# Attention-bias kernel on one core: zero fills, parameter transfer, distance sign and coefficient columns at the start rearranged

## Chip, cores and metric

The kernel runs on 1 core of one Trainium2 chip. The metric is the device time of one launch in microseconds (us), and the time of a kernel is the median of its runs. Times inside the program are counted from the start of the profiled span.

## What is computed

Attention with a learned relative-position bias, followed by two feed-forward stages. Sizes: batch 2, 8 heads, 576 positions, head size 64, hidden width 32 of the bias network, then 1152 tokens by 512 features and 2048 inner features.

```python
scores = scale * np.matmul(q, k.transpose(0, 1, 3, 2))
psi_rel = np.log1p(np.abs(pos[:, None] - pos[None, :]))
psi_i = np.log1p(np.maximum(pos[:, None], 1.0))
x = (psi_rel / psi_i)[..., None]
h = np.maximum(x @ w1 + b1, 0.0)
scores = scores + (h @ w2).transpose(2, 0, 1)[None]
attn = softmax(scores)
x = attn @ v                        # then to (tokens, features)
h = x @ w_in;  x = (P(h) / Q(h)) @ w_out        # first feed-forward stage
h = x @ w_in2; out = np.maximum(0.01 * h, h) @ w_out2
```

## The kernel before

**Stages.** The program first makes the bias for all heads and positions ("bias stage", up to about 85 us), then runs attention unit by unit over (head pair, batch), then the two feed-forward stages on TensorE. The order of every engine's work is written out by hand in lists (`BIAS_PLAN`, `EXTRA`, `PLAN`, `TAIL`, `START`) or computed before the launch by a planner (`plan_first`); no list depends on measured time. The change touches what comes ahead of the first mask, and the two calls that make the bias columns.

**How the bias is made.** For a hidden unit the ReLU is linear on either side of one distance, so the kernel turns it into a comparison of a signed distance with a threshold. A table `z` (128 x 1152, f16) holds distances for 32 hidden units in each of 4 partition groups; it is loaded by ACT's queue (L613) and multiplied by the sign `sg` of the hidden weight on ScalarE (L628). The thresholds `thr` and `nthr` (128 x 144) come from a short chain on VectorE: `sg` (L626, L627), `aw`, `rate` (L629 to L633), `thr` (L652, L653), an Exp on ScalarE (L654), then `thr` and `nthr` (L655, L656).

For each of the 36 row groups n, `b_mask` makes 4 masks (one for each c) from `z`: on VectorE with `thr` (L689), or on ScalarE with `nthr` (L687), as the letters of `MASKS[n % 4]` say ('A' for ScalarE). `b_mm` multiplies masks by the coefficients `coef` on TensorE into two PSUM tiles (L697). `b_t0` on ScalarE (L709) scales the first by `rows_e` and adds a column of `ca_i`; `b_t1` on GpSimd (L715) multiplies by `te`; `b_out` on VectorE (L720) adds the second and a column of `cab`, and SyncE's queue writes the tile to its place (L723). `BIAS_PLAN` orders these for each n; masks run 3 to 4 groups ahead.

**The parameters.** One transfer on SP's queue (L611) brings `par`, 128 rows of 348 f32 (174 KB): `wc` (2 columns), `wflat` (32), `w2rep` (128), the feed-forward scalars (6), `rows_z` (144) and `rows_e` (36). Behind it on that queue are the two halves of `te` (L614, L615) and `sm` (L616). From `wc` GpSimd makes `nwc` and `hwc` (L635, L637). ScalarE makes four pieces of `c32` (L647) and their f16 part `coef` (L648); GpSimd makes the rest (L649). One small matmul fills `psc` (L641).

**`cab` and `ca_i`.** `cab` (128 x 4 x 2) is zeroed on GpSimd (L639). `cab_constants()` runs on VectorE between the first VectorE masks and the rest: for each of the 4 mask patterns it copies the ScalarE quarters out of `psc` (6 copies in all, L670) and multiplies `rows_e` by a column (4 times, L671).

**The zero fills.** Two tiles `qz` of 128 x 2 x 1152 hold the queries of a unit, with zeros where a head's rows meet the other head's columns. GpSimd writes these zeros with four fills of 64 x 1152 (L660, L661), issued in program order behind the coefficient work, and then `ones`, `tiny` and `ln15` (L662 to L664). The queries are put in by `prep_q`, later in the bias stage.

Of the kernel before, what the change touches and what calls it, by code (L numbers as in the profile page):

```python
# [9 lines left out]
F32 = mybir.dt.float32  # L10
# [16 lines left out]
MASKS = ('AVVA', 'VVVA', 'VVAA', 'VVVA')  # L27
# [88 lines left out]
HI_MERGED = ()  # L116
LO_MERGED = ()
REM_MERGED = (0, 1)
PAR = 168 + S // 4 + NG
GROUPS = [[(0, 0), (0, 1)], [(1, 0), (1, 1)], [(3, 0), (3, 1)], [(2, 0), (2, 1)], [(8, 2)]]  # L120
GROUPS_END = [[(0, 0), (0, 1)], [(1, 0), (1, 1)], [(3, 0), (3, 1)], [(2, 0), (2, 1)], [(8, 2)]]
GROUPS_0 = [[(2, 0), (2, 1)], [(0, 0), (0, 1)], [(1, 0), (1, 1)], [(3, 0), (3, 1)], [(8, 2)]]
# [145 lines left out]
def host_constants():  # L268
    psi = np.log1p(np.arange(S, dtype=np.float32))
    psi_i = np.log1p(np.maximum(np.arange(S, dtype=np.float32), np.float32(1.0)))  # L270
    p = np.arange(128)
    c = np.arange(2 * S)
    g = p // HID
    e = p // H

    def away(off):
        return np.abs(c[None, :] - S - off[:, None])

    dist = away(4 * g).astype(np.float16)
    tabs = psi[np.minimum(away(4 * e), S - 1)].astype(np.float32)  # L280
    first = np.array([first_row(n) for n in range(NG)])
    first_z = (first[:, None] + 16 * np.arange(4)[None, :]).reshape(-1)
    rows_z = psi_i[4 * g[:, None] + first_z[None, :]]
    rows_e = np.float32(1.0) / psi_i[4 * e[:, None] + first[None, :]]
    eye = np.eye(128)
    m = np.concatenate([np.arange(8), [-1, 8, -1]]).repeat(64)
    k = np.arange(128)[:, None]
    rows = np.concatenate([rows_z, rows_e], 1).astype(np.float32)
    small = np.concatenate([eye, k == m[None, :]], 1).astype(np.float32)
    return rows, {  # L290
        "dist": np.ascontiguousarray(dist),
        "tabs": np.ascontiguousarray(tabs),
        "small": np.ascontiguousarray(small),
    }
# [3 lines left out]
def attn_bias_moe_kernel(  # L298
# [16 lines left out]
    V, A, G, PE, SP = nc.vector, nc.scalar, nc.gpsimd, nc.tensor, nc.sync  # L315
# [285 lines left out]
    with ExitStack() as st:  # L601
# [3 lines left out]
        psa = st_s.enter_context(tc.tile_pool(name="psa", bufs=2, space=PSUM, side="right"))  # L605
        psb = st.enter_context(tc.tile_pool(name="psb", bufs=2, space=PSUM))

        pr = b1p.tile([128, PAR], F32, name="par")
        z = b1p.tile([128, 2 * S], F16, name="z")
        te = b1p.tile([128, 2 * S], F32, name="te")  # L610
        SP.dma_start(out=pr, in_=par)  # L611
        halves = (slice(512, 2 * S), slice(0, 512))
        A.dma_start(out=z, in_=dist)  # L613
        SP.dma_start(out=te[:, halves[0]], in_=tabs[:, halves[0]])  # L614
        SP.dma_start(out=te[:, halves[1]], in_=tabs[:, halves[1]])  # L615
        SP.dma_start(out=sm, in_=small)  # L616
        wc, wflat, w2rep = pr[:, 0:2], pr[:, 2:34], pr[0:HID, 34:162]
        rows_z, rows_e = pr[:, 168:168 + S // 4], pr[:, 168 + S // 4:PAR]

        def col1(nm):
            return b1p.tile([128, 1], F32, name=nm)

        sg, aw, rate = col1("sg"), col1("aw"), col1("rate")
        V.tensor_scalar(sg, wc[:, 0:1], 0.0, 2.0, ALU.is_ge, ALU.mult)  # L626
        V.tensor_scalar(sg, sg, -1.0, None, ALU.add)  # L627
        A.activation(z, z, AF.Copy, scale=sg)  # L628
        V.tensor_scalar(aw, wc[:, 0:1], sg, 1e-30, ALU.mult, ALU.max)  # L629
        V.reciprocal(aw, aw)  # L630
        V.tensor_tensor(rate, sg, wc[:, 1:2], ALU.mult)
# [3 lines left out]
        G.tensor_scalar(nwc, wc, -1.0, None, ALU.mult)  # L635
        hwc = b1p.tile([128, 2], F32, name="hwc")
        G.tensor_scalar(hwc, wc, -0.5, None, ALU.mult)  # L637
        cab = b1p.tile([128, len(MASKS), 2], F32, name="cab")
        G.memset(cab, 0.0)  # L639
        psc = psa.tile([128, 1024], F32, tag="A", name="psc")  # L640
        PE.matmul(psc[:, 0:2], w2rep, hwc[0:HID, :], start=True, stop=True)  # L641

        coef = b1p.tile([128, 2, 2, 2, 4 * H], F16, name="coef")
        c32 = b1p.tile([128, 2, 2, 4 * H], F32, name="c32")
        for m, src in enumerate((nwc, hwc)):
            for j in range(2):
                A.activation(c32[:, m, j], wflat, AF.Copy, scale=src[:, j:j + 1])  # L647
        A.activation(coef[:, :, :, 0], c32, AF.Copy)  # L648
        G.tensor_tensor(coef[:, :, :, 1], c32, coef[:, :, :, 0], ALU.subtract)  # L649
        thr = b1p.tile([128, S // 4], F32, name="thr")  # L650
        nthr = b1p.tile([128, S // 4], F32, name="nthr")
        V.tensor_scalar(thr, rows_z, rate, 7.3, ALU.mult, ALU.min)  # L652
        V.tensor_scalar(thr, thr, -13.2, None, ALU.max)  # L653
        A.activation(thr, thr, AF.Exp)  # L654
        V.tensor_scalar(thr, thr, -1.0, sg, ALU.add, ALU.mult)  # L655
        V.tensor_scalar(nthr, thr, -1.0, None, ALU.mult)  # L656
        ca_i = b1p.tile([128, len(MASKS), NG], F32, name="ca_i")

        for u in range(2):
            G.memset(qz[u][0:64, :, S:2 * S].bitcast(F32), 0.0)  # L660
            G.memset(qz[u][64:128, :, 0:S].bitcast(F32), 0.0)  # L661
        G.memset(ones, 1.0)  # L662
        G.memset(tiny, 1e-30)
        G.memset(ln15, float(15 * np.log(2)))  # L664

        def cab_constants():
            for x in range(len(MASKS)):
                for y in range(4):
                    if MASKS[x][y] == "A":
                        V.tensor_copy(cab[32 * y:32 * y + 32, x], psc[32 * y:32 * y + 32, 0:2])  # L670
                V.tensor_scalar(ca_i[:, x], rows_e, cab[:, x, 0:1], None, ALU.mult)  # L671

        def late_constants():
            V.memset(onep, 1.0 + 1e-6)
            A.activation(ab, pr[:, 162:168], AF.Copy)
            A.activation(babs, ab[:, 4:6], AF.Abs)
            V.tensor_scalar(nab, ab[:, 0:4], -1.0, None, ALU.mult)

# [599 lines left out]
```

## Time and profile before

| | before |
|---|---|
| median of 3 runs | 681.64 us (679.17 to 682.61) |
| profiled execution, its own time | 683.32 us |
| its span | 681.5 us |
| mean granted TensorE clock | 0.96 |
| busy share of the span: PE, DVE, ACT, POOL | 88%, 77%, 59%, 55% |

PE is TensorE, DVE is VectorE, ACT is ScalarE, POOL is GpSimd, SP is SyncE. A busy share is a mean over stages that have different limits. A row of the timeline gives the start, the length, engine, line and operation, what it writes and reads, how many instructions are merged in it, and in brackets the idle time in front of it with what ended that. The granted clock is 1.00 for the upper of TensorE's two levels (2.4 GHz) and 0.50 for the lower (1.2 GHz).

### The profile page before, as it was taken

Reading aid. Unit: us, or ns where it says so; the run is one execution under the profiler, and the core shown is the slowest. Engines: PE = TensorE matmul, PEld = TensorE weight load, DVE = VectorE, ACT = ScalarE, POOL = GpSimd, SP = SyncE. Lnnn points to the kernel's source line nnn. Section 1 sums busy time; section 2 is a strip of 40 time slices with the busy share of each in tenths; the row PEclk is TensorE's granted clock in tenths of the full one; section 3 lists DMA queues with packets and bytes.
Section 4 is the critical chain, followed back from the end, with each engine's and each line's share of the span. In section 5 each row is a group of like instructions: output and inputs, shape, how many; then the busy total and the mean of one; then the engine's idle time right before and its main releaser. Section 6 shows DMA issues by size and latency. Waiting matters only on the chain.

```text
span 681.5 us, 11805 instructions
## 1 busy us (share of the span) xinstructions
PE 599.9 (88%) x4595; PEld 530.3 (78%) x4595; DVE 527.4 (77%) x815; ACT 402.4 (59%) x614; POOL 376.8 (55%) x276
## 2 busy tenths in 40 slices
PE   2777678998888877579999999999999999999998
PEld 1343467777677876579999898999999999998876
DVE  6999788888789857988999999899355465645463
ACT  5999677786687556688576776854244323232210
POOL 4678667787688711456556575853055534453340
PEclk9999889898999887779999999999999999999999
DMA  2666769999999931213211311011033312230113
GB/s 87 176 178 153 202 127 199 201 207 172 188 200 201 199 105 65 92 63 114 72 63 63 123 63 63 31 60 66 15 118 115 124 63 91 94 125 31 55 54 124
DMA packets 104359, 77.35 MB, mean 113 GB/s; under 512 B 86512, under 2 KB 86896, under 8 KB 104304
## 3 DMA queue, kind: packets, MB, share of 16 engines
q1 hardware_dynamic: 100704, 68.97, 40.1%
q10 hardware_dynamic: 3600, 7.64, 3.8%
q8 instruction: 36, 0.59, 0.4%
q14 instruction: 19, 0.16, 0.1%
HBM read 42.38 MB, written 2.36 MB: 66 GB/s over the span
## 4 chain that ended last, share of the span: by engine, by line
PE 43%; DVE 26%; ACT 11%; DMA 8%; issue 7%; POOL 3%; ACTq 1%; SPq 0%; DVEq 0%; POOLq 0%
PE ph L426 19%; PE pz L1049 13%; DMA et<-hl 6%; PE py L1008 6%; ACT mk L687 2%; DVE raw L387 2%; DVE raw L385 2%; DVE raw L383 2%; POOL hl L854 2%; DVE ph L479 2%; DVE bias L1020 2%; ACT t L709 2%; DVE s L500 2%; DVE qq L470 2%; DVE pt L801 2%
## 5 line engine op out<-in xcount | busy, mean ns | idle before, releaser
L426 PE MATMUL ph<-bias,bias 128*128 128x384 f32 x1152 | 217.8, 344 | 15.8 <-DVE s L500 13.2
L426 PEld LDWEIGHTS ph<-bias,bias 128*128 128x128 f32 x1152 | 208.8, 194 | 21.3 <-issue 13.2
L854 POOL TENSOR_TENSOR hl<-ex,hl 128x512 f16<-128x512 f32 (+2 forms) x105 | 105.1, 1018 | 34.0 <-DVE hl L841 17.7
L521 POOL TENSOR_TENSOR gl<-s,gh 128x1152 fp32r<-128x1152 f32 (+1 forms) x33 | 85.5, 2595 | 34.9 <-ACT gh L516 34.4
L789 PE MATMUL ps<-kt,qz 128*128 128x288 f32 x432 | 82.9, 336 | 16.8 <-DVE mn L801 9.2
L405 POOL TENSOR_TENSOR bias<-raw,bias 128x512 fp32r<-128x512 f32 x37 | 49.1, 1330 | 73.3 <-ACT bias L397 70.0
L789 PEld LDWEIGHTS ps<-kt,qz 128*128 128x128 f32 x432 | 67.1, 210 | 28.2 <-DVE mn L801 12.6
L1008 PE MATMUL py<-gh,wo 128*128 128x384 f32 x288 | 80.5, 340 | 3.8 <-DVE bias L1020 3.1
L1057 DVE TENSOR_TENSOR bias<-pz,bias 128x512 f32<-128x512 f32 x48 | 33.1, 689 | 59.6 <-PE pz L1049 59.4
L1049 PE MATMUL pz<-wo,gh 128*128 128x512 f32 (+1 forms) x240 | 74.4, 386 | 0.3 <-DVE bias L1057 0.3
L405 POOL TENSOR_TENSOR wo<-raw,wo 128x512 fp32r<-128x512 f32 x23 | 30.3, 1315 | 78.6 <-ACT wo L397 78.6
L697 PEld LDWEIGHTS <-coef 128*32 128x32 f16 x1152 | 27.2, 100 | 47.8 <-issue 31.6
L817 ACT ACTIVATE ex<-pt,mn 128x576 f32<-128x576 f32 x72 | 55.2, 766 | 14.2 <-DVE mn L801 12.3
L715 POOL TENSOR_TENSOR t<-t,te 128x576 f32<-128x576 f32 x36 | 48.9, 1361 | 19.3 <-ACT t L709 8.5
L1008 PEld LDWEIGHTS py<-gh,wo 128*128 128x128 f32 x288 | 52.6, 188 | 7.5 <-DVE bias L1020 5.6
L801 DVE CUSTOM_DVE_ANT_0 pt<-ps,bias 128x576 f32<-128x576 f32 x64 | 47.8, 748 | 6.4 <-PE ps L789 4.3
L1008 PE MATMUL py<-gl,wo 128*128 128x384 f32 x156 | 52.2, 335 | 0.0
L397 ACT ACTIVATE wo<-raw 128x512 fp32r<-128x512 f32 x27 | 17.0, 629 | 58.3 <-DVE raw L387 58.3
L1049 PEld LDWEIGHTS pz<-wo,gh 128*128 128x128 f32 x240 | 44.2, 188 | 8.2 <-DVE bias L1057 0.7
L508 ACT ACTIVATE s<-ph 128x1152 f32<-128x1152 f32 x16 | 18.2, 1137 | 54.5 <-PE ph L426 43.3
L1049 PE MATMUL pz<-wo,gl 128*128 128x512 f32 (+1 forms) x129 | 50.1, 388 | 0.0
L497 POOL TENSOR_TENSOR qq<-qq,r 128x1152 f32<-128x1152 f32 (+1 forms) x15 | 38.0, 2530 | 16.6 <-ACT r L486 12.0
(133 smaller groups left out, 1184.8 us busy)
## 6 DMA issues: line engine op xcount, KB each, us to landing
biasr<-in_moe_w_in SPq DMA_DIRECT2D x32, 512.0 KB, 4.5
biasr<-in_moe_w_out SPq DMA_DIRECT2D x32, 512.0 KB, 3.6
bias<-bb SPq DMA_DIRECT2D x32, 288.0 KB, 3.6
vl<-in_v ACTq DMA_DIRECT2D x8, 320.0 KB, 4.0
ql<-in_q ACTq DMA_DIRECT2D x8, 288.0 KB, 4.5
kl<-in_k ACTq DMA_DIRECT2D x8, 288.0 KB, 4.9
out<-bias SPq DMA_DIRECT2D x8, 256.0 KB, 2.0
biasr<-bb SPq DMA_DIRECT2D x8, 144.0 KB, 2.9
```

Of the source, the lines that this page charges most:

```text
L405: G.tensor_tensor(lo_, raw[:, x], hi_.bitcast(F32), ALU.subtract)
L426: PE.matmul(ps[:, c, 0:CH], w[:, sl], x[kk][:, c * CH:(c + 1) * CH], start=(kk == 0 and n == 0), stop=(kk == KD - 1 and n == 2),)
L497: G.tensor_tensor(part(qq[f], c), part(qq[f], c), part(r0[f], c), ALU.mult)
L521: eng.tensor_tensor(part(gl, c), part(s1[f], c), part(gh, c).bitcast(F32), ALU.subtract)
L715: G.tensor_tensor(t1, t0s.pop(n), te[:, S - first_row(n):2 * S - first_row(n)], ALU.mult)
L789: PE.matmul(ps[:, c, 0:288], lt[:, a], kts[i][:, b, 288 * c:288 * c + 288], start=(n == 0), stop=(n == 2),)
L801: V.tensor_tensor_reduce(out=c2(pt), in0=s_ps.pop((i, j))[:, :, 0:288], in1=c2(bsrc), op0=ALU.add, op1=ALU.min, scale=1.0, scalar=3.0e38, ...
L817: A.activation(et, pt, AF.Exp, bias=mn, scale=-1.0, accum_out=sums[i][:, col:col + 1],)
L854: engines[j in at].tensor_tensor(hl[:, xs, dst], e9[:, xs, src], hl[:, xs, src], ALU.subtract)
L1008: PE.matmul(ps[:, 0:CH], w[:, sl], gts[f][x][:, cs], start=(f == f0 and m == 0), stop=(f == f0 + nf - 1 and m == 2),)
L1049: PE.matmul(ps[:, half], gts[f][x][:, sl], w[:, half], start=(f == f0 and m == 0), stop=(f == f0 + nf - 1 and m == 2),)
L1057: V.tensor_tensor(dst, ps[:, half], dst, ALU.add)
```

## The change

`par` comes in two transfers on the same queue: a head of 34 columns (`wc`, `wflat`; tile `hd`) and the rest (tile `par`), which gets four more columns, `picks`, that hold 1 or 0 for "this quarter is ScalarE's in this pattern". All zero fills move ahead of the parameter work in program order; those of `qz[0]` stay on GpSimd, and those of `qz[1]` become two copies on ScalarE from a column of zeros read as a broadcast. `z` is multiplied by its sign on VectorE, behind the first two `thr` operations, and no longer on ScalarE. The Exp of `thr` moves between the two pairs of `c32` copies. The 10 operations of `cab_constants` become two products with broadcast operands.

```diff
-PAR = 168 + S // 4 + NG
+HEAD = 34
+PAR = 168 + S // 4 + NG + len(MASKS)
...
-        pr = b1p.tile([128, PAR], F32, name="par")
+        hd = b1p.tile([128, HEAD], F32, name="hd")
+        pr = b1p.tile([128, PAR - HEAD], F32, name="par")
...
-        SP.dma_start(out=pr, in_=par)
+        SP.dma_start(out=hd, in_=par[:, 0:HEAD])
+        SP.dma_start(out=pr, in_=par[:, HEAD:PAR])
...
-        wc, wflat, w2rep = pr[:, 0:2], pr[:, 2:34], pr[0:HID, 34:162]
-        rows_z, rows_e = pr[:, 168:168 + S // 4], pr[:, 168 + S // 4:PAR]
+        wc, wflat, w2rep = hd[:, 0:2], hd[:, 2:34], pr[0:HID, 0:128]
+        c0, c1 = 134 + S // 4, 134 + S // 4 + NG
+        rows_z, rows_e, picks = pr[:, 134:c0], pr[:, c0:c1], pr[:, c1:]
...
+        zero = col1("zero")
+        G.memset(zero, 0.0)
+        G.memset(qz[0][0:64, :, S:2 * S].bitcast(F32), 0.0)
+        G.memset(qz[0][64:128, :, 0:S].bitcast(F32), 0.0)
+        for r, c in ((slice(0, 64), slice(S, 2 * S)), (slice(64, 128), slice(0, S))):
+            A.activation(qz[1][r, :, c], zero[r].unsqueeze(2).broadcast_to([64, 2, S]), AF.Copy)
+        G.memset(ones, 1.0)
+        G.memset(tiny, 1e-30)
+        G.memset(ln15, float(15 * np.log(2)))
...
-        A.activation(z, z, AF.Copy, scale=sg)
...
-        cab = b1p.tile([128, len(MASKS), 2], F32, name="cab")
-        G.memset(cab, 0.0)
...
         V.tensor_scalar(thr, thr, -13.2, None, ALU.max)
-        A.activation(thr, thr, AF.Exp)
+        V.tensor_scalar(z, z, sg, None, ALU.mult)
+        for m, src in enumerate((nwc, hwc)):
+            for j in range(2):
+                A.activation(c32[:, m, j], wflat, AF.Copy, scale=src[:, j:j + 1])
+            if m == 0:
+                A.activation(thr, thr, AF.Exp)
+        A.activation(coef[:, :, :, 0], c32, AF.Copy)
+        G.tensor_tensor(coef[:, :, :, 1], c32, coef[:, :, :, 0], ALU.subtract)
         V.tensor_scalar(thr, thr, -1.0, sg, ALU.add, ALU.mult)
...
-        for u in range(2):
-            G.memset(qz[u][0:64, :, S:2 * S].bitcast(F32), 0.0)
-            G.memset(qz[u][64:128, :, 0:S].bitcast(F32), 0.0)
-        G.memset(ones, 1.0)
-        G.memset(tiny, 1e-30)
-        G.memset(ln15, float(15 * np.log(2)))
...
         def cab_constants():
-            for x in range(len(MASKS)):
-                for y in range(4):
-                    if MASKS[x][y] == "A":
-                        V.tensor_copy(cab[32 * y:32 * y + 32, x], psc[32 * y:32 * y + 32, 0:2])
-                V.tensor_scalar(ca_i[:, x], rows_e, cab[:, x, 0:1], None, ALU.mult)
+            n = len(MASKS)
+            V.tensor_tensor(
+                cab, picks.unsqueeze(2).broadcast_to([128, n, 2]), psc[:, 0:2].unsqueeze(1).broadcast_to([128, n, 2]), ALU.mult
+            )
+            V.tensor_tensor(
+                ca_i, rows_e.unsqueeze(1).broadcast_to([128, n, NG]), cab[:, :, 0:1].broadcast_to([128, n, NG]), ALU.mult
+            )
```

## Rows read from the trace of the kernel before

**Rows 1.** The page's first line.

```profile
span 681.5 us, 11805 instructions
```

**Rows 2.** The chain that ended last, its start: start, length, what.

```profile
0.74 3.46 DMA par<-in_par
...
10.72 1.13 DVE ca_i L671
```

**Rows 3.** Busy time by stretch (x instructions), then granted clock, DMA share, GB/s.

```profile
10.00:20.00 10.00, 6.97 (x116) 2.96 (x119) 9.71 (x27) 7.74 (x12) 5.96 (x8) 1.00 0.02 5
20.00:40.00 20.00, 13.86 (x357) 7.95 (x346) 19.88 (x41) 19.64 (x31) 13.54 (x12) 1.00 0.80 208
40.00:60.00 20.00, 15.03 (x352) 8.55 (x346) 19.94 (x40) 19.92 (x31) 15.49 (x12) 1.00 0.60 155
```

**Rows 4.** Timeline of all engines, 0 to 9.6 us.

```profile
0.73 1.28 ACT L317 ACT_TABLE_LOAD   x1 [0.73 <-PEq L1266]
...
1.19 0.42 SPq L614 DMA_DIRECT2D te<-in_tabs  x1
...
4.22 0.15 DVE L626 TENSOR_SCALAR sg<-par 128x1 f32<-128x1 f32 x1 [4.22 <-DMA par<-in_par]
...
4.60 1.25 ACT L628 ACTIVATE z<-z,sg 128x1152 f16<-128x1152 f16 x1 [2.59 <-DVE sg L627]
...
5.49 0.30 DVE L652 TENSOR_SCALAR thr<-par,rate 128x144 f32<-128x144 f32 x1
5.76 0.52 ACT L647 ACTIVATE c<-par,nwc 128x32 f32<-128x32 f32 x2
5.82 0.23 DVE L653 TENSOR_SCALAR thr<-thr 128x144 f32<-128x144 f32 x1
...
6.74 0.31 ACT L648 ACTIVATE coef<-c 128x128 f16<-128x128 f32 x1
...
7.13 0.42 POOL L649 TENSOR_TENSOR coef<-c,coef 128x128 f16<-128x128 f32 x1 [2.42 <-ACT coef L648]
7.29 1.34 DVE L655 TENSOR_SCALAR thr<-thr,sg 128x144 f32<-128x144 f32 x1 [1.24 <-ACT thr L654]
7.49 1.05 POOL L660 MEMSET qz<- 64x1152 f32 x1
...
8.67 1.05 DVE L656 TENSOR_SCALAR nthr<-thr 128x144 f32<-128x144 f32 x1
```

**Rows 5.** Timeline of all engines, 9.6 to 18 us.

```profile
9.64 0.80 DVE L689 TENSOR_SCALAR mk<-z,thr 128x576 f16<-128x576 f16 x2
...
9.76 2.77 ACT L687 ACTIVATE mk<-z,nthr 128x576 f16<-128x576 f16 x4 [2.50 <-DVE nthr L656]
10.37 0.32 DVE L670 COPY cab<-psc 32x2 f32<-32x2 f32 x2
...
10.72 1.13 DVE L671 TENSOR_SCALAR ca_i<-par,cab 128x36 f32<-128x36 f32 x1
...
12.44 0.81 ACT L709 ACTIVATE t<-psA,ca_i,par 128x576 f32<-128x576 f32 x1
...
13.36 4.30 DVE L689 TENSOR_SCALAR mk<-z,thr 128x576 f16<-128x576 f16 x10
...
15.96 0.83 ACT L709 ACTIVATE t<-psA,ca_i,par 128x576 f32<-128x576 f32 x1 [2.05 <-PE psA L697]
...
17.69 0.82 DVE L720 SCALAR_TENSOR_TENSOR bb<-psB,cab,t 128x576 f32<-128x576 f32 x1
```

**Rows 6.** DMA issues of the whole page: size, us from issue to landing.

```profile
out<-bias SPq DMA_DIRECT2D x8, 256.0 KB, 2.0
```

**Rows 7.** DMA issues of 0 to 30 us: size, us from issue to landing.

```profile
te<-in_tabs SPq DMA_DIRECT2D x1, 320.0 KB, 4.0
```

**Rows 8.** Busy time by stretch, columns as in rows 3, 260 to 280 us.

```profile
260.00:264.00 4.00, 3.90 (x12) 3.64 (x13) 3.40 (x6) 2.02 (x5) 0.00 (x0) 0.50 0.02 4
...
276.00:280.00 4.00, 1.48 (x5) 1.51 (x6) 3.69 (x3) 1.14 (x4) 1.98 (x1) 0.50 0.11 44
```

More of the change, by code (lines that the diff above doesn't have):

```diff
@@ L287, in host_constants @@
     k = np.arange(128)[:, None]
-    rows = np.concatenate([rows_z, rows_e], 1).astype(np.float32)
+    picks = np.array([[pat[y] == "A" for pat in MASKS] for y in range(4)]).repeat(32, 0)
+    rows = np.concatenate([rows_z, rows_e, picks], 1).astype(np.float32)
     small = np.concatenate([eye, k == m[None, :]], 1).astype(np.float32)
@@ L644, in attn_bias_moe_kernel @@
         c32 = b1p.tile([128, 2, 2, 4 * H], F32, name="c32")
[L645 to L649, printed above, removed]
         thr = b1p.tile([128, S // 4], F32, name="thr")
@@ L653, in attn_bias_moe_kernel @@
         V.tensor_scalar(thr, thr, -13.2, None, ALU.max)
-        A.activation(thr, thr, AF.Exp)
+        V.tensor_scalar(z, z, sg, None, ALU.mult)
[6 more added lines that the diff above has]
+        G.tensor_tensor(coef[:, :, :, 1], c32, coef[:, :, :, 0], ALU.subtract)
         V.tensor_scalar(thr, thr, -1.0, sg, ALU.add, ALU.mult)
         V.tensor_scalar(nthr, thr, -1.0, None, ALU.mult)
+        cab = b1p.tile([128, len(MASKS), 2], F32, name="cab")
         ca_i = b1p.tile([128, len(MASKS), NG], F32, name="ca_i")
-        for u in range(2):
-            G.memset(qz[u][0:64, :, S:2 * S].bitcast(F32), 0.0)
-            G.memset(qz[u][64:128, :, 0:S].bitcast(F32), 0.0)
-        G.memset(ones, 1.0)
-        G.memset(tiny, 1e-30)
-        G.memset(ln15, float(15 * np.log(2)))
-        def cab_constants():
-            for x in range(len(MASKS)):
-                for y in range(4):
-                    if MASKS[x][y] == "A":
-                        V.tensor_copy(cab[32 * y:32 * y + 32, x], psc[32 * y:32 * y + 32, 0:2])
-                V.tensor_scalar(ca_i[:, x], rows_e, cab[:, x, 0:1], None, ALU.mult)
+        def cab_constants():
+            n = len(MASKS)
[5 more added lines that the diff above has]
+            )
         def late_constants():
             V.memset(onep, 1.0 + 1e-6)
-            A.activation(ab, pr[:, 162:168], AF.Copy)
+            A.activation(ab, pr[:, 128:134], AF.Copy)
             A.activation(babs, ab[:, 4:6], AF.Abs)
```

## The prediction

> **What bounds the kernel now.** I read the page first: the span is 681.5 us [rows 1]. The profiled execution took 683.32 us, so 1.8 us lie around the span, and it is 1.7 us above the median of the runs shown, 681.64. I work against 683.32 and take the difference off the median.
>
> Next I read the chain of waits from its beginning. It starts with the transfer of the parameters, 3.46 us from issue to landing, and soon rests on VectorE pieces that write small constant columns, such as 1.13 us for a 36-column product [rows 2]. The reader is to see that the whole program hangs on this beginning; but whether a microsecond saved there is still there at the end depends on what follows. So the third view is busy time by stretch: from 20 to 60 us VectorE is busy 39.8 of 40 us and ScalarE 39.6 of 40, while TensorE and GpSimd have slack; from 10 to 20 us VectorE is busy 9.7 and ScalarE 7.7 [rows 3]. Both engines are full for the rest of the bias stage, with work that the change doesn't touch. If both start that work earlier, the stage ends earlier by the smaller of their two leads.
>
> Last I read the timeline of the first 18 us, which tells how each engine gets to its first mask. VectorE waits until 4.22 for the parameters. Then two things stand out [rows 4]. The third and fourth threshold operations (L655, L656) take 1.34 and 1.05 us, where the same shape took 0.23 (L653): while they run, GpSimd is at its coefficient product (0.42 us from 7.13) and then at four fills of 1.05 us each from 7.49. I read that as VectorE held by GpSimd. ScalarE's first mask at 9.76 waits for exactly that, 2.5 us of idle time ended by L656 [rows 5]. After the first two masks VectorE spends 10.37 to 13.36 on `cab_constants`, and ScalarE's second `t` operation at 15.96 has 2.05 us of idle time ended by TensorE, which itself waited for the masks behind `cab_constants` [rows 5].
>
> **The change part by part.**
>
> *Parameters in two transfers.* The head has a tenth of the bytes of the old one and the same place in the queue. No row has so small a load. It lands at best 2.0 us after its issue at 0.74, the shortest landing on the page [rows 6], so at 2.74, and at worst like the old one, at 4.20 [rows 2]. I take the middle, 3.5. The rest is issued one slot later, where `te` was, at 1.19 [rows 4]; with the old 3.46 us it lands at 4.65, with the 4.0 of `te` [rows 7] at 5.19, and at best at 4.20. I take 4.7. Three transfers are moved one slot of 0.45 us down SP's queue: `te`'s first half then lands near 5.6, its second a slot later, and the first reader (L715) comes after the first `t`, near 9.3 by the sum below. `sm` is wanted much later. All three cost nothing; had the cover gone, it would be 0.45 us.
>
> *VectorE up to `thr`.* From `sg` to L652 it needs 4.22 to 5.49, that is 1.27 us [rows 4]; from 3.5 this ends at 4.8, just behind the second transfer. L652 and L653 take until 6.05 in the old count, 0.56 us, so `thr` is ready for the Exp at 5.35.
>
> *Sign of `z` on VectorE.* It is 1152 f16 columns; a mask of half that length takes 0.40 [rows 5], so by rows 0.80, from 5.35 to 6.15. The Trainium skill, "VectorE: DVE Perf Modes", section "What auto-detection actually checks", says that a single-source operation with dense 16-bit source and destination of even outer size runs at four elements a cycle; a mask, written into padded rows, isn't dense, so the rule would put this product at about 0.4 us as an estimate. No run so far shows such an operation; by that rule thresholds and sum would come out 0.1 to 0.3 us better. I keep the 0.80 of the rows.
>
> *ScalarE.* Its table load ends at 2.01 [rows 4]. The two fills of 1152 columns each have no row; the nearest is the old product of `z`, also 1152 columns, 1.25 us. That makes 2.5 us, until 4.5, in time in which ScalarE did nothing before (it idled 2.59 us ahead of 4.60). At best they cost nothing; at worst, read twice as slowly for the broadcast and the wider type, 5.0 us until 7.0. I take 2.5. The 1.25 us of `z` go. Then two `c32` copies take 0.52, to 5.05, and the Exp waits for `thr` until 5.4. Queued behind the waiting Exp are only two more copies and `coef`; who waits for those is TensorE, and it lacks masks until later. Exp to 5.7 (0.31, as `coef`), copies to 6.2, `coef` to 6.5.
>
> *The held thresholds.* L655 starts behind `z` at 6.15 and, with no fill on GpSimd, takes 0.23; so does L656. Both are done by 6.6. GpSimd's four fills are now two, right after the start, over by about 2.7 (two of 1.05 behind some short ones), before the head lands. First VectorE mask at 6.6 instead of 9.64, first ScalarE mask at 6.65 instead of 9.76: **both lead by 3.1 us**.
>
> What can be late next is L656: GpSimd's coefficient product (0.42) now starts at about 6.5, and if it comes first, L656 waits for it as L655 did. I take no hold, since L656 starts before that by the sum, and put 0.4 us into the range. The Trainium skill, "GPSIMD Engine Reference", section "8. Key points", says that GpSimd contends with VectorE instructions in a two-port mode or with two SBUF inputs. The slow L655 and L656 agree with its first half (1.34 and 1.05 against 0.23); the second half no row here shows, and by it the new `ca_i` product, with two SBUF inputs, could be held too and end the sum 0.1 us worse, if GpSimd's 0.42 us fell on it.
>
> *Two products for `cab` and `ca_i`.* The old ten operations take 10.37 to 13.36, that is 2.99 us [rows 5]. The new ones have 8 and 144 columns. The nearest rows are a copy out of `psc` at 0.16 and L652 with 144 columns at 0.30; both ends are near, 0.45 to 0.9, since a product may run at half the pace of L652. I take 0.55. VectorE starts its ten masks 3.1 + 2.4 = **5.5 us earlier**, at 7.9 instead of 13.36, and reaches its first `bb` (17.69) with that lead.
>
> *ScalarE behind that.* Its first four masks and the first `t` follow at the old spacing: `t` at 12.44 − 3.1 = 9.3, the next mask, the second `t` at 10.8 at the earliest (0.7 for the `t`, 0.77 for the mask), while TensorE delivers at 15.96 − 5.5 = 10.5. So it is now ScalarE itself that is last, at 10.8 against 15.96: **a lead of 5.2 us**. The 2.05 us of idle time are gone, and no more can be gained here.
>
> *Sum.* VectorE leads by 5.5, ScalarE by 5.2, and both are full afterwards [rows 3]; the smaller counts. Own time: 683.3 − 5.2 = 678.1; from the median, 681.6 − 5.2 = **676.4 us**.
>
> Bounds: with the head at 4.20 the thresholds are 0.7 us later, and with L656 held 0.4 more: a lead of 4.1. With both transfers at their best `thr` is ready at 4.8, but ScalarE's fills and first copies end at 5.05, so only 0.3 us more is had: 5.5. That makes 676.1 to 677.5 for the mechanism alone.
>
> **The rivals.** A change of 0.5%, 3.4 us, is about what a measurement of this kernel can tell from none; so faster means under 678.2.
>
> *Only the first lead lasts.* If the masks behind `cab_constants` weren't what held ScalarE and TensorE, the shorter constants would only leave VectorE idle later, and 3.1 us would remain: 678.5. For it: TensorE and GpSimd have waits of their own in this stage. Against it: VectorE has no idle time between 10.37 and 17.69 and is full to 60 us.
>
> *The fills are slow.* At 5.0 us for both, ScalarE's copies start at 7.0, the Exp at 7.5, the Exp ends at 7.8 and ScalarE, behind two more copies and `coef`, masks from 8.7. Its first lead shrinks to 1.0; with the 2.05 us of idle time gone that is 3.1 at its second `t`, so 678.5. Against it: the width of 1.25 us for 1152 columns; for it: no row with a broadcast input. That the change doesn't do what it says would show here, the fills only being moved onto the path.
>
> *The clock at the hand-over.* Between attention and the first feed-forward stage TensorE has gaps and was granted the lower of its two levels: 0.50 in 260 to 264 and in 276 to 280 [rows 8]. Four microseconds at that level give up 2 us of TensorE's work. If the earlier start made the gaps fall otherwise, five more such stretches would cost 10 us: 676.4 + 10 = 686.4, slower. It decides from 5.2 us on, that is from the third such stretch on. Against it: behind the bias stage every engine's order is the same and all of it moves alike, so that the gaps move with it.
>
> **How the numbers follow.** The forecast gets 0.70; the first rival 0.15, the second 0.08, the third 0.07. The runs shown spread from 2.5 below their median to 1.0 above; put on the bounds, the likely case reaches from 674.3 to 678.5, and the two milder rivals with the same spread end near 679.8. So the range is 674.3 to 679.8, which leaves out the third rival and the tails. Faster: nearly nine tenths of the forecast, a third of the two milder rivals, 0.70. Slower: most of the third, 0.05. The rest, 0.25, is no change that can be told.
>
> **What would show each step.** In the new timeline the `hd` load should release `sg` before 4 us; no GpSimd fill should start after 3 us; L655 and L656 of old should take about 0.23 each; the first masks should begin near 6.6 on both engines; the constants should take two operations of some 0.5 us in all; and the first `bb` should come near 12.2. By stretch, VectorE and ScalarE should be full from about 11 us on, and the end of the bias stage 5 us earlier. The prediction is wrong if the fills end later than 5.4 on ScalarE, if the second transfer lands after 5.5, or if the lead at the first `bb` is there and gone at the first attention tile.

## The result, and the profile after

The changed kernel takes 675.86 us (median of 17 runs) where the kernel before takes 682.61 (17 runs, the three shown earlier among them). The ratio is 0.9907, 95% interval 0.9879 to 0.9935, so it is faster by 6.3 us (4.4 to 8.3). The ratio goes by the means of the runs, without one run of the changed kernel (683.26 us) that fell into a slower state; the medians differ by 6.75 us. The forecast was 676.4 us, 5.2 us less than the 681.6 that were shown.

The page's first line of the changed kernel; its own time was 675.86 us, so again 1.8 us lie around the span:

```profile
span 674.1 us, 11797 instructions
```

DMA issues of the first 25 us of the changed kernel (size, us from issue to landing):

```profile
par<-in_par SPq DMA_DIRECT2D x1, 159.0 KB, 3.1
hd<-in_par SPq DMA_DIRECT2D x1, 17.0 KB, 2.7
```

The timeline of all engines, 2 to 12 us, which answers to [rows 4] and [rows 5] (line numbers are those of the changed kernel):

```profile
2.01 2.33 ACT L633 ACTIVATE qz<-zero 64x1152 fp32r<-64x1152 f32 x2
...
3.44 0.15 DVE L639 TENSOR_SCALAR sg<-hd 128x1 f32<-128x1 f32 x1 [3.44 <-DMA hd<-in_par]
...
4.06 0.16 DVE L642 RECIPROCAL aw<-aw 128x1 f32<-128x1 f32 x1
4.14 0.14 DVE L643 TENSOR_TENSOR rate<-sg,hd 128x1 f32<-128x1 f32 x1
4.32 0.16 DVE L644 SCALAR_TENSOR_TENSOR rate<-rate,aw 128x1 f32<-128x1 f32 x1
4.35 0.53 ACT L662 ACTIVATE c<-hd,nwc 128x32 f32<-128x32 f32 x2
...
4.70 0.30 DVE L657 TENSOR_SCALAR thr<-par,rate 128x144 f32<-128x144 f32 x1
5.03 0.23 DVE L658 TENSOR_SCALAR thr<-thr 128x144 f32<-128x144 f32 x1
5.18 0.51 DVE L659 TENSOR_SCALAR z<-z,sg 128x1152 f16<-128x1152 f16 x1
5.30 0.32 ACT L664 ACTIVATE thr<-thr 128x144 f32<-128x144 f32 x1 [0.41 <-DVE thr L658]
...
5.66 0.29 DVE L667 TENSOR_SCALAR thr<-thr,sg 128x144 f32<-128x144 f32 x1
5.98 0.23 DVE L668 TENSOR_SCALAR nthr<-thr 128x144 f32<-128x144 f32 x1
...
6.13 0.92 DVE L697 TENSOR_SCALAR mk<-z,thr 128x576 f16<-128x576 f16 x2
6.29 2.76 ACT L695 ACTIVATE mk<-z,nthr 128x576 f16<-128x576 f16 x4
...
6.47 0.43 POOL L666 TENSOR_TENSOR coef<-c,coef 128x128 f16<-128x128 f32 x1 [2.58 <-ACT coef L665]
6.98 0.15 DVE L674 TENSOR_TENSOR cab<-par,psc 128x8 f32<-128x8 f32 x1
...
7.17 0.31 DVE L677 TENSOR_TENSOR ca_i<-par,cab 128x144 f32<-128x144 f32 x1
7.39 4.29 DVE L697 TENSOR_SCALAR mk<-z,thr 128x576 f16<-128x576 f16 x10
...
10.34 0.82 ACT L717 ACTIVATE t<-psA,ca_i,par 128x576 f32<-128x576 f32 x1
...
11.61 0.81 DVE L728 SCALAR_TENSOR_TENSOR bb<-psB,cab,t 128x576 f32<-128x576 f32 x1
```

The reader is to see three things. The two late threshold operations (L667, L668; L655 and L656 of the kernel before) take 0.29 and 0.23 us instead of 1.34 and 1.05. `cab` and `ca_i` are made between 6.98 and 7.39, in 0.41 us instead of 2.99. And the idle time in front of ScalarE's second `t` is gone: it starts at 10.34, straight behind a mask. VectorE leads by 3.5 us at its first mask and by 6.1 at its first `bb` (17.69 − 11.61), ScalarE by 5.6 at its second `t` (15.96 − 10.34).

Busy time by stretch, columns as in [rows 3]:

```profile
10.00:20.00 10.00, 8.69 (x203) 5.73 (x199) 9.95 (x22) 10.00 (x16) 7.87 (x6) 1.00 0.51 138
20.00:40.00 20.00, 14.03 (x346) 7.97 (x342) 19.78 (x40) 19.62 (x33) 13.65 (x11) 1.00 0.72 188
40.00:60.00 20.00, 14.38 (x333) 7.89 (x333) 19.94 (x39) 19.95 (x30) 16.18 (x12) 1.00 0.62 163
```

ScalarE, busy for 7.74 of 10 us between 10 and 20 us before, is now busy for all of them; from 20 us on both engines are as full as they were. So the lead travels through a stretch in which neither engine has idle time to swallow it. How far it travels is told by four landmarks: the start of VectorE's first `bb`, of ScalarE's second `t`, of the first attention matmul, and of the last `pz` matmul. They are given for the two kernels and for all experiments below. The attention matmuls run in the order of the code, so the first one marks the end of the bias stage. Beside them stands the start of `sg`, VectorE's first operation, which waits for the parameters to land, and how far behind it the first `bb` starts.

| kernel | `sg` | first `bb` | `bb` behind `sg` | second `t` | first attention matmul | last matmul | time against before, 95% interval |
|---|---|---|---|---|---|---|---|
| before | 4.22 | 17.69 | 13.47 | 15.96 | 84.4 | 678.2 | |
| changed | 3.44 | 11.61 | 8.17 | 10.34 | 77.5 | 670.8 | 0.9907 (0.9879 to 0.9935) |
| changed, again | 3.33 | 11.50 | 8.17 | 10.23 | 78.0 | 673.3 | 0.9918 (0.9883 to 0.9952) |
| before + fills | 4.10 | 14.99 | 10.89 | 13.27 | 82.7 | 675.7 | 0.9973 (0.9947 to 1.0) |
| before + products | 4.11 | 14.88 | 10.77 | 13.70 | 82.2 | 671.4 | 0.9954 (0.9922 to 0.9987) |
| before + both | 4.17 | 13.24 | 9.07 | 11.95 | 79.1 | 668.6 | 0.9917 (0.9879 to 0.9956) |
| changed, fills back | 3.31 | 12.77 | 9.46 | 10.21 | 79.9 | 674.9 | 0.9937 (0.9910 to 0.9963) |
| changed, old columns | 3.13 | 13.11 | 9.98 | 11.39 | 79.7 | 675.5 | 0.9956 (0.9929 to 0.9982) |
| changed, one transfer | 3.91 | 12.08 | 8.17 | 10.82 | 79.6 | 676.4 | 0.9941 (0.9909 to 0.9972) |
| changed, `z` on ScalarE | 3.15 | 12.23 | 9.08 | 10.96 | 79.4 | 669.5 | 0.9946 (0.9906 to 0.9987) |
| changed, four fills on ScalarE | 3.52 | 13.18 | 9.66 | 11.92 | 80.4 | 669.9 | 0.9951 (0.9925 to 0.9977) |
| changed, three more fills | 3.54 | 13.36 | 9.82 | 12.07 | 80.1 | 674.3 | 0.9974 (0.9945 to 1.0002) |
| changed, `rate` in one operation | 3.19 | 11.36 | 8.17 | 10.09 | 78.7 | 672.2 | 0.9928 (0.9888 to 0.9967) |

All columns but the last are from one profiled execution each. The last matmul wanders: "before + both" comes to it 2.11 us ahead of the changed kernel, though its bias stage ends 1.6 us behind. The first attention matmul wanders too, by over 1 us: "`rate` in one operation" has its first `bb` 0.25 us ahead of the changed kernel and its first attention matmul 1.2 us behind. And `sg` starts when the transfer lands, which differs from trace to trace: 3.13 to 3.54 in the eight with a head, 3.91 to 4.22 in the five with one transfer. So parts are judged by the first `bb` and the second `t`, to a tenth of a microsecond only when both are counted from `sg`, and the time only by the last column.

### The profile page after: what moved, and what is told of

The parts are those of the page before. It is cut to its first block, busy times and chain, and to the rows that moved or that the text cites. A ratio compares the mean times of both kernels' runs of the same rounds, so it can differ in the third digit from the quotient of the medians.

```text
span 674.1 us, 11797 instructions
## 1 busy us (share of the span) xinstructions
PE 594.7 (88%) x4595; PEld 527.4 (78%) x4595; DVE 521.6 (77%) x808; ACT 403.8 (60%) x615; POOL 376.4 (56%) x274
## 4 chain that ended last, share of the span: by engine, by line
PE 42%; DVE 30%; ACT 11%; DMA 8%; issue 6%; POOL 2%; ACTq 1%; SPq 0%; DVEq 0%; POOLq 0%
PE ph L428 20%; PE pz L1057 13%; PE py L1016 5%; DMA et<-hl 4%; DVE raw L389 3%; DVE bias L1028 2%; ACT ex L825 2%; DVE raw L387 2%; DVE ph L481 2%; ACT mk L695 2%; DVE raw L385 2%; DVE mk L697 2%; DVE s L502 2%; DVE pt L809 2%; DVE s L505 2%
## 5 line engine op out<-in xcount | busy, mean ns | idle before, releaser
L428 PE MATMUL ph<-bias,bias 128*128 128x384 f32 x1152 | 215.3, 341 | 16.5 <-DVE s L502 13.8
L428 PEld LDWEIGHTS ph<-bias,bias 128*128 128x128 f32 x1152 | 206.0, 192 | 22.3 <-issue 13.8
L797 PE MATMUL ps<-kt,qz 128*128 128x288 f32 x432 | 80.5, 330 | 16.9 <-DVE mn L809 8.1
L797 PEld LDWEIGHTS ps<-kt,qz 128*128 128x128 f32 x432 | 65.6, 207 | 27.6 <-DVE mn L809 11.6
```

The source lines that it names most:

```text
L428: PE.matmul(ps[:, c, 0:CH], w[:, sl], x[kk][:, c * CH:(c + 1) * CH], start=(kk == 0 and n == 0), stop=(kk == KD - 1 and n == 2),)
L797: PE.matmul(ps[:, c, 0:288], lt[:, a], kts[i][:, b, 288 * c:288 * c + 288], start=(n == 0), stop=(n == 2),)
```

## The experiments

**Does the lead come back, and is it the lead that decides the time?** The changed kernel, unaltered, once more.

> The changed kernel as it is, a second time, to see how far one profiled execution differs from another. My theory: the landmarks of the bias stage come back within 0.4 us (first masks near 6.1 and 6.3, first bb near 11.6, second t near 10.3) and the first attention matmul within 1.5 us of 77.5, while the end may differ by several us with the granted clock behind the attention stage; median 6 us under before. Rival (the lead is lost or gained behind the bias stage by the change itself): end and first attention matmul move together with the first bb.

The first masks, `bb` and `t` came back within 0.11 us, and `sg` had started 0.11 earlier: counted from `sg` the first `bb` is at 8.17 us in both traces. The first attention matmul came 0.55 us later and the last matmul 2.59, with the time 5.6 us less than before (0.9918, 3.3 to 8.0). So the start of a trace can be trusted to a tenth of a microsecond from `sg` on, and its end to a few. A like spread is seen over all runs of the changed kernel, and it goes with the clock: the eight with a mean granted clock of 0.964 or more took 671.05 to 675.86 us, the five with 0.957 or less took 676.92 to 680.82, and the four between them 673.95 to 683.26. The kernel before shows the same: of its 30 runs beside "before + fills", the eight with 0.964 or more took 675.58 to 682.82 us, the fourteen with 0.957 or less 682.85 to 688.58. So within one kernel executions differ by more than the change is worth, and the longer ones mostly have the lower clock; whether the clock makes them longer no run here shows.

**The fills alone, on the kernel before** (`ones`, `tiny` and `ln15` move with them).

```diff
+        zero = col1("zero")
+        G.memset(zero, 0.0)
+        G.memset(qz[0][0:64, :, S:2 * S].bitcast(F32), 0.0)
+        G.memset(qz[0][64:128, :, 0:S].bitcast(F32), 0.0)
+        for r, c in ((slice(0, 64), slice(S, 2 * S)), (slice(64, 128), slice(0, S))):
+            A.activation(qz[1][r, :, c], zero[r].unsqueeze(2).broadcast_to([64, 2, S]), AF.Copy)
...
-        for u in range(2):
-            G.memset(qz[u][0:64, :, S:2 * S].bitcast(F32), 0.0)
-            G.memset(qz[u][64:128, :, 0:S].bitcast(F32), 0.0)
```

> The kernel before with one part of the change alone: all zero fills, ones, tiny and ln15 ahead of the parameters, two of the four qz fills on ScalarE. My theory (VectorE was held by GpSimd's fills): the third threshold operation still meets GpSimd's coefficient product and takes up to 0.5 us, the fourth takes 0.23 instead of 1.05, the first ca_i product 0.24 instead of 1.13. First VectorE mask near 8.0 (before 9.64), first bb near 15.1 (before 17.69), second t of ScalarE near 13.4 (15.96), first attention matmul near 81.8 (84.4), time 2.6 us less. Rival (these operations were slow for a reason of their own, the fills only stood beside them): thresholds stay at 1.3 and 1.05, first bb within 0.3 of 17.7, time the same.

The timeline of this kernel, 7 to 14 us:

```profile
7.01 0.43 POOL L659 TENSOR_TENSOR coef<-c,coef 128x128 f16<-128x128 f32 x1 [2.42 <-ACT coef L658]
7.17 0.35 DVE L665 TENSOR_SCALAR thr<-thr,sg 128x144 f32<-128x144 f32 x1 [1.24 <-ACT thr L664]
7.56 0.24 DVE L666 TENSOR_SCALAR nthr<-thr 128x144 f32<-128x144 f32 x1
...
8.91 0.24 DVE L675 TENSOR_SCALAR ca_i<-par,cab 128x36 f32<-128x36 f32 x1
...
13.27 0.83 ACT L713 ACTIVATE t<-psA,ca_i,par 128x576 f32<-128x576 f32 x1 [1.28 <-PE psA L701]
```

Same operations, same inputs, no fill beside them: 0.35, 0.24 and 0.24 us instead of 1.34, 1.05 and 1.13. The first meets GpSimd's coefficient product, which ends at 7.44, and ends 0.08 us behind it; in the changed kernel it takes 0.29. The first `bb` comes 2.70 us earlier, where 2.6 was expected (2.58 counted from `sg`), and the rival, that these operations were slow by themselves, falls. The time moved by 1.8 us (0 to 3.6), which is just at the edge of what can be told from none. ScalarE's second `t` still waits 1.28 us for the masks behind the ten column operations, which is what the other part is for.

**The two products alone, on the kernel before** (with `picks` as four more columns of the one transfer, and `cab_constants` as in the change).

> The kernel before with one part of the change alone: cab and ca_i by two broadcast products. The fills stay on GpSimd behind the coefficient work, so they still run beside the products. My theory: first VectorE mask unchanged at 9.6; the two products take 0.5 us where ten operations took 2.99; first bb near 15.2, second t near 13.5, first attention matmul near 82, time 2.5 us less. If a product with two SBUF inputs is held by a fill too, ca_i takes 0.5 to 1.4 us, first bb 15.6 to 16.4. Rival (only the lead at the first mask lasts): first bb earlier, but the first attention matmul within 0.5 of 84.4 and the time the same.

The timeline of this kernel, 7 to 11 us:

```profile
7.17 1.34 DVE L656 TENSOR_SCALAR thr<-thr,sg 128x144 f32<-128x144 f32 x1 [1.24 <-ACT thr L655]
...
8.54 1.05 DVE L657 TENSOR_SCALAR nthr<-thr 128x144 f32<-128x144 f32 x1
...
9.55 1.05 POOL L661 MEMSET qz<- 64x1152 f32 x1
...
10.25 0.14 DVE L669 TENSOR_TENSOR cab<-par,psc 128x8 f32<-128x8 f32 x1
10.43 0.31 DVE L672 TENSOR_TENSOR ca_i<-par,cab 128x144 f32<-128x144 f32 x1
```

The thresholds are as late as before, the columns take 0.4 us, and the first `bb` comes 2.81 us earlier (2.5 expected; 2.70 counted from `sg`), the first attention matmul 2.2. The rival, that only the lead at the first mask lasts, falls: here there is hardly a lead at the first mask (9.52 against 9.64), and 3.1 us (0.9 to 5.3) are gone from the time.

**Both, on the kernel before.**

> The kernel before with fills moved and constants by two products; one transfer, z on ScalarE and the order of Exp stay as before. My theory: the two parts add up: first VectorE mask near 8.0, constants 0.5 us, first bb near 13.4 (4.3 less), second t near 11.9, first attention matmul 4 to 4.5 us earlier, time 4 to 4.5 us less; the rest of the change (transfers, z, Exp) is then worth some 1.5 to 2 us. Rival (the clock at the hand-over decides the time): the landmarks of the bias stage move but the time does not follow them.

First `bb` 4.45 us earlier (4.3 expected), second `t` 4.0, first attention matmul 5.3, time 5.7 us less (3.0 to 8.3). Counted from `sg`, two parts that gain 2.58 and 2.70 by themselves give 4.40 together, not 5.28: the 0.89 us by which a fill held one of the old `ca_i` products (1.13 for 0.24) is in both. By the landmarks these two parts are three quarters of the lead (4.45 of 6.08 us). The rest, 1.63, is 0.73 of earlier landing (`sg` at 3.44 for 4.17) and 0.90 behind `sg`. The run with `z` back on ScalarE, below, gives 0.91 for that, so the Exp's new place seems worth nothing beside it; no run tests that place by itself. The rival falls at the first attention matmul and in the time, though within an interval of 5 us.

**The columns undone, on the changed kernel** (`cab` zeroed on GpSimd early, `cab_constants` as before).

> The changed kernel with the ten old operations for cab and ca_i (cab zeroed on GpSimd early). No fill runs beside them, so each takes its short time: 2.1 us in all where the two products take 0.41. First masks unchanged at 6.1 and 6.3, first bb near 13.3 (changed kernel 11.61), second t near 11.9 (10.34), first attention matmul near 79 (77.5), time 1.5 us more than the changed kernel. Rival (only the lead at the first mask lasts): first attention matmul and time as in the changed kernel.

The ten operations, held by nothing, took from 6.68 to 8.78, 2.1 us as expected, and the first `bb` came at 13.11 (13.3 expected). `sg` had started at 3.13 here, 0.31 us earlier than in the changed kernel's trace, so that counted from `sg` the old columns cost 1.8 us at the first `bb` and 1.4 at the second `t`. This kernel's ScalarE row shows the wait come back:

```profile
11.39 0.83 ACT L716 ACTIVATE t<-psA,ca_i,par 128x576 f32<-128x576 f32 x1 [1.25 <-PE psA L704]
```

The first attention matmul is at 79.7, 2.26 us behind the changed kernel's, so the rival falls as far as one trace can tell. The time is 3.0 us under before (1.2 to 4.8), with the lead of 4.57 us inside that.

**The fills undone, on the changed kernel** (all four on GpSimd, behind the coefficient product).

> The changed kernel with the zero fills back behind the coefficient work, all four on GpSimd. They now run from about 6.9 to 11.2, behind the thresholds (done at 6.2), so no threshold operation is held: first masks stay at 6.1 and 6.3. Two things remain: the ca_i product at 7.2 has two SBUF inputs and meets the first fill; if such a product is held, it takes about 0.9 us instead of 0.31, if not, 0.3. And GpSimd's first t is queued behind the fills: it starts near 11.5 instead of 9.85, so the first bb comes near 12.9 instead of 11.61 and VectorE waits for it. Time 1.3 us more than the changed kernel, 5 us less than before. Rival (the fills themselves are what the change gains by): first masks back near 8 to 9, time 3 us more than the changed kernel.

The timeline of this kernel, 6 to 13 us:

```profile
6.70 1.05 POOL L664 MEMSET qz<- 64x1152 f32 x1
...
7.03 0.31 DVE L675 TENSOR_TENSOR ca_i<-par,cab 128x144 f32<-128x144 f32 x1
7.26 4.30 DVE L695 TENSOR_SCALAR mk<-z,thr 128x576 f16<-128x576 f16 x10
...
11.32 2.79 POOL L721 TENSOR_TENSOR t<-t,te 128x576 f32<-128x576 f32 x2
12.77 0.82 DVE L726 SCALAR_TENSOR_TENSOR bb<-psB,cab,t 128x576 f32<-128x576 f32 x1 [1.22 <-POOL t L721]
```

Three answers. The product of two SBUF inputs, wholly inside a fill, takes 0.31 us, as it does without one: it is not held. Nor are the ten masks, which run beside the fills (the last fill ends at 11.02): 4.30 us, where they took 4.29 in the changed kernel. So a fill doesn't hold every VectorE operation. And with the thresholds out of the fills' way, moving the fills still gains 1.2 us at the first `bb` (12.77, 12.9 expected), for another reason than on the kernel before: GpSimd's own first `t` is queued behind them, and VectorE's first `bb` waits 1.22 us for it. The first masks stay at 6.0 and 6.2, so the rival falls; the second `t` is no later, and the time (0.9937) doesn't tell this kernel from the changed one. What a part is worth depends on what else has been changed.

**One transfer again, on the changed kernel** (`hd` and `par` are then two parts of one tile, `both`).

```diff
-        SP.dma_start(out=hd, in_=par[:, 0:HEAD])
-        SP.dma_start(out=pr, in_=par[:, HEAD:PAR])
+        SP.dma_start(out=both, in_=par)
```

> The changed kernel with the parameters in one transfer again. It lands near 4.2, so sg starts at 4.2 instead of 3.44 and thr is ready 0.7 us later; ScalarE's first copies wait as well. First masks near 6.8 and 7.0, first bb near 12.3, first attention matmul near 78.2, time 0.7 us more, which the rounds will hardly tell. Rival (the transfer is hidden behind ScalarE's fills): first masks unchanged.

The row of `sg` in this kernel's timeline:

```profile
3.91 0.15 DVE L638 TENSOR_SCALAR sg<-par 128x1 f32<-128x1 f32 x1 [3.91 <-DMA par<-in_par]
```

It starts at 3.91 instead of 3.44, and first masks, `bb` (12.08) and `t` (10.82) are 0.47 or 0.48 us later; the first `bb` is 8.17 us behind `sg`, as in the changed kernel. Expected were 0.7, but this time the transfer landed sooner than the 4.20 of [rows 2]. The split is worth its earlier landing, no more: over all traces `sg` starts at 3.33 in the mean of the eight with a head and at 4.10 in the mean of the five with one transfer, 0.77 us apart. The time, 0.9941, tells nothing of so little.

**`z` on ScalarE again, on the changed kernel** (the old line, between `sg` and `aw`).

> The changed kernel with z multiplied on ScalarE behind its fills, as before. 1.25 us more in ScalarE's queue from 4.35: copies from 5.6, Exp near 6.2, coef done near 7.2. First VectorE mask near 7.0 (6.13), first ScalarE mask near 7.2 (6.29), first bb near 12.5, second t near 11.2, time 0.9 us more. Rival (z costs the same on either engine): landmarks unchanged.

The timeline of this kernel, two rows:

```profile
4.35 1.25 ACT L641 ACTIVATE z<-z,sg 128x1152 f16<-128x1152 f16 x1
...
6.28 0.29 DVE L667 TENSOR_SCALAR thr<-thr,sg 128x144 f32<-128x144 f32 x1 [1.30 <-ACT thr L664]
```

ScalarE's queue is longer by 1.25 us, the Exp comes late, and VectorE waits 1.30 us for it: first mask at 6.76, `bb` at 12.23, 0.62 us later (0.9 expected; `sg` had started 0.29 earlier, so against the landing it is 0.91). In the changed kernel the same product takes 0.51 us on VectorE, in time in which VectorE waits for the Exp anyway.

**Twice the fills on ScalarE, on the changed kernel**, which prices the rival of slow fills.

```diff
-        G.memset(qz[0][0:64, :, S:2 * S].bitcast(F32), 0.0)
-        G.memset(qz[0][64:128, :, 0:S].bitcast(F32), 0.0)
...
-            A.activation(qz[1][r, :, c], zero[r].unsqueeze(2).broadcast_to([64, 2, S]), AF.Copy)
+            for u in range(2):
+                A.activation(qz[u][r, :, c], zero[r].unsqueeze(2).broadcast_to([64, 2, S]), AF.Copy)
```

> The changed kernel with all four qz fills on ScalarE, 4.7 us instead of 2.33, from 2.0 to 6.7. This prices the rival of slow fills: the copies start at 6.7 instead of 4.35, the Exp at 7.3 instead of 5.3; first VectorE mask near 8.1 (6.13), first ScalarE mask near 8.6 (6.29), first bb near 13.6, second t near 12.7 (10.34), first attention matmul near 79.6, time 2.2 us more. Rival (ScalarE has slack there): first masks within 0.5 us of the changed kernel.

Its timeline has the fills until 6.44 and the copies right behind:

```profile
2.01 4.43 ACT L632 ACTIVATE qz<-zero 64x1152 fp32r<-64x1152 f32 x4
...
6.45 0.53 ACT L661 ACTIVATE c<-hd,nwc 128x32 f32<-128x32 f32 x2
```

`bb` at 13.18 and second `t` at 11.92, both 1.6 us later, where 2.0 and 2.4 were expected. The 2.1 us of added fills took away the 0.41 us for which the Exp had waited before they cost anything. So two fills are free on ScalarE and four are not; had each of the two taken twice as long, the gain would have been 4.0 us at the second `t` instead of 5.6.

**A fill put where it hurts, on the changed kernel.**

```diff
         G.tensor_scalar(hwc, wc, -0.5, None, ALU.mult)
+        G.memset(qz[0][0:64, :, S:2 * S].bitcast(F32), 0.0)
+        G.memset(qz[0][64:128, :, 0:S].bitcast(F32), 0.0)
+        G.memset(qz[0][0:64, :, S:2 * S].bitcast(F32), 0.0)
```

> The changed kernel with three more fills of 64x1152 on GpSimd behind hwc (they write the same zeros again), from about 3.95 to 7.1, across the threshold operations and the product of z. If a fill holds single-source VectorE operations: the first threshold operation (alone 0.30) ends only behind the first fill near 5.1, the second (0.23) takes about 1.0, the product of z (0.51) about 1.0; first VectorE mask near 7.7 instead of 6.13, first bb near 13.2, time 1.6 us more. If fills don't hold them, the durations stay at 0.30, 0.23 and 0.51 and the first masks at 6.1 and 6.3; only the coefficient product on GpSimd is late, 7.1 instead of 6.5.

The timeline of this kernel, 3.9 to 8 us:

```profile
3.92 1.05 POOL L650 MEMSET qz<- 64x1152 f32 x1
...
4.80 0.29 DVE L660 TENSOR_SCALAR thr<-par,rate 128x144 f32<-128x144 f32 x1
5.02 1.07 POOL L651 MEMSET qz<- 64x1152 f32 x1
5.13 1.05 DVE L661 TENSOR_SCALAR thr<-thr 128x144 f32<-128x144 f32 x1
6.10 0.39 DVE L662 TENSOR_SCALAR z<-z,sg 128x1152 f16<-128x1152 f16 x1
6.14 1.34 POOL L652 MEMSET qz<- 64x1152 f32 x1
...
6.57 1.00 DVE L670 TENSOR_SCALAR thr<-thr,sg 128x144 f32<-128x144 f32 x1
...
7.46 0.42 POOL L669 TENSOR_TENSOR coef<-c,coef 128x128 f16<-128x128 f32 x1
7.61 0.37 DVE L671 TENSOR_SCALAR nthr<-thr 128x144 f32<-128x144 f32 x1
```

The first threshold operation ends 0.12 us behind the first fill, but at its usual 0.29 us, so it tells nothing. The second, 0.23 us by itself, runs from 5.13 to 6.18, to just behind the end of the fill (6.09), and the third from 6.57 to 7.57, behind the fill's 7.48. The fourth meets the coefficient product and takes 0.37 for 0.23, ending 0.10 us behind it. The `z` product did what I hadn't expected: it started 0.04 us ahead of the third fill, took 0.39 us, and the fill took 1.34 us instead of 1.05. Of these, the one that starts first holds the other. First mask at 7.90, `bb` at 13.36 (13.2 expected). The time lies 1.8 us under before (−0.1 to 3.8); the lead of 3.9 us at the second `t` is just outside.

**One operation less in front of the thresholds, on the changed kernel.**

```diff
-        V.tensor_tensor(rate, sg, wc[:, 1:2], ALU.mult)
-        V.scalar_tensor_tensor(rate, rate, -1.0, aw, ALU.mult, ALU.mult)
+        V.scalar_tensor_tensor(rate, wc[:, 1:2], sg, aw, ALU.mult, ALU.mult)
...
-        V.tensor_scalar(thr, rows_z, rate, 7.3, ALU.mult, ALU.min)
-        V.tensor_scalar(thr, thr, -13.2, None, ALU.max)
+        V.tensor_scalar(thr, rows_z, rate, -7.3, ALU.mult, ALU.max)
+        V.tensor_scalar(thr, thr, 13.2, None, ALU.min)
...
-                A.activation(thr, thr, AF.Exp)
+                A.activation(thr, thr, AF.Exp, scale=-1.0)
```

> The changed kernel with one VectorE operation less ahead of the thresholds: rate in one operation instead of two, its sign taken into the Exp's scale. The chain from hd to the first masks is what both engines wait for by my theory, so every landmark should come 0.2 us earlier against the landing of hd: first mask 2.5 us behind sg instead of 2.69, first bb 8.0 us behind it instead of 8.17. Time 0.2 us less, which no rounds can tell. Rival (ScalarE's fills and copies bind): first masks unchanged against the end of the fills.

A miss, and the landmarks show it without any timing. `sg` starts at 3.19 in this trace and `bb` at 11.36, 8.17 us later, exactly as in the changed kernel (11.61 − 3.44). Two rows of its timeline say why:

```profile
3.82 0.16 DVE L642 RECIPROCAL aw<-aw 128x1 f32<-128x1 f32 x1
4.01 0.22 DVE L643 SCALAR_TENSOR_TENSOR rate<-hd,sg,aw 128x1 f32<-128x1 f32 x1
```

The first mask moved with `sg`, from 6.13 to 5.89, so the rival falls as well: ScalarE's queue doesn't bind here. In the changed kernel the operation that was taken out starts 0.08 us behind the reciprocal, which it doesn't need, and the next starts 0.26 us behind the reciprocal, which it does. Now that next one starts 0.19 us behind it and takes 0.06 us longer. By these starts the removed operation stood almost wholly in a wait.

## Why the prediction was right, point by point

**What bounds.** Right. Both engines were full from the start to 70 us in both kernels (from 60 to 70 us each is busy 10.0 of 10; from 70 to 80, in the kernel before, VectorE 9.1 and ScalarE 8.4). The smaller lead, ScalarE's, was forecast as 5.2 us and is 5.6 in the trace, and the time fell by 6.3 us (4.4 to 8.3), an interval that holds both. Which of the two leads counts, VectorE's 6.1 or ScalarE's 5.6, it cannot tell, nor can the first attention matmul, which came 6.9 and 6.4 us earlier in the two traces of the changed kernel. The forecast was a fall of 5.2 us from 681.6; the fall was larger and the kernel before, in 17 runs, 1.0 us slower than shown, and the two partly cancel: that 675.86 comes so close to 676.4 is in part luck. The likely case was added up wrongly at its lower end, too (676.1 − 2.5 is 673.6, not 674.3); nothing hangs on it.

**VectorE held by GpSimd's fills.** Shown from both sides: without the fills the operations take 0.24 to 0.35 us (before + fills), with them put back in the way 1.0 us again (three more fills). One price was not seen: of the 1.13 us of the first `ca_i` product [rows 2] a fill's hold was 0.89. L656, feared to be late behind the coefficient product, was not: it ran at 5.98, the product at 6.47. The sentence drawn from the Trainium skill, "GPSIMD Engine Reference", section "8. Key points", is borne out by these runs in its first half for the `f32` threshold operations and the `z` product; masks weren't held. Of its second half, two SBUF inputs, the run with the fills undone shows the opposite beside a fill, which only writes (0.31 us), and the measurement decides; beside GpSimd work that reads no run tests it.

**The transfers.** The head was put at 3.5 and landed at 3.4; the rest was put at 4.7 and landed 3.1 us after 1.18, at 4.3. VectorE never waited for it, so that its chain ran on by itself. The undone split gives 0.5 us where the sum had 0.7, and the means over all traces 0.77.

**`z` on VectorE.** The 0.80 us of the rows was the worse price. It took 0.51 us in the changed kernel, of which 0.08 overlap the operation in front, and 0.39 in the run with three more fills, right behind a held operation. A mask of half the columns is shown with 0.50 us in the same trace, and with 0.39 behind the held L656 of the kernel before; the 0.80 doubled a row that has this short one in it. So like for like the product took no longer than a mask of half its columns. The Trainium skill, "VectorE: DVE Perf Modes", section "What auto-detection actually checks", gave 0.4 as an estimate, and here its rule was the better guide than a row of another shape. By the prediction's own sum it would have put the thresholds 0.4 us earlier, not 0.1 to 0.3, and VectorE's first mask did come at 6.13 for 6.6. Most of the product lay beside the Exp.

**ScalarE.** The fills took 2.33 us for the 2.5 of the sum, and the Exp waited 0.41 us for `thr`, as forecast; nothing that hung behind the waiting Exp was missed. The rival of slow fills was not what happened, and its price was nearly right: 2.5 us more of fills were to cost 2.1, and 2.1 more cost 1.6.

**The two products.** 0.41 us for 0.55. The lead at the ten masks is 6.0 instead of 5.5; 0.4 of the difference was there at the first mask already (3.5 for 3.1).

**From the lead to the end.** The first rival, that only the lead at the first mask lasts, falls with "before + products". The third, the clock at the hand-over, doesn't decide the sign: from the first attention matmul to the last matmul it is 593.8 us before, 593.3 and 595.3 in the two traces of the changed kernel, and 589.2 to 596.8 over all thirteen. The argument against this rival, that all of it moves alike, isn't borne out, though: the stretch differs by 2.0 us between two executions of one kernel. Within one kernel executions differ by over 9 us, and the longer ones mostly show the lower granted clock. That the parts' leads are what the time follows is supported, not proved in detail: in ten of the eleven experiments and in the changed kernel the smaller of the two leads lies inside the interval of the measured time, but these intervals are 3.5 to 5.5 us wide, and in nine of the twelve the time fell by less than the lead, by 0.1 to 2.1 us. That all of a lead reaches the end isn't shown, and single parts of half a microsecond can't be told by time at all.

## What to carry to other kernels

Look at operations whose duration is far above that of the same shape elsewhere in the trace, and at what another engine does in exactly that stretch: work without a deadline, such as zero fills, belongs where the engines wait for the first transfer. Follow a lead by landmarks, counted from the arrival that starts the chain: so counted they come back to a tenth of a microsecond, while the arrival itself differs by some tenths. Use the whole time only for the sum of the parts. Before an operation is removed from a chain, see whether its successor starts earlier without it, or only waits longer for something else.

## What the runs showed of the hardware

- A GpSimd fill of 64x1152 f32 (1.05 us) holds a VectorE `tensor_scalar` of 128x144 f32 to its end: 0.23 us became 1.05, ending 0.09 us behind the fill. The other way about, the fill became 1.34 us behind a `tensor_scalar` of 128x1152 f16 (0.39) that had started 0.04 us earlier.
- It doesn't hold every `tensor_scalar`: ten masks of 128x576 f16, written into padded rows, took 4.30 us beside fills and 4.29 without.
- GpSimd's coefficient product (128x128, 0.43 us) holds a threshold operation in the same way: 0.23 us became 0.37, ending 0.10 behind it.
- A VectorE product of two SBUF inputs (128x144 f32) ran in 0.31 us inside such a fill, undisturbed.
- A ScalarE copy of a broadcast column into 64x1152 f32 goes at the pace of a plain one: two took 2.33 us and four 4.43, where one plain 1152-column product took 1.25.
- A load of 17 KB in rows of 136 bytes landed 2.4 to 2.8 us after its issue in eight traces; one of 174 or 176 KB in its place, in five others, 3.2 to 3.5.
